# First tiles of four sequences moved to the front of a fused attention and feed-forward kernel

## The chip, the cores and the metric

The kernel runs on one core of a Trainium2 chip. The core has a matrix engine (TensorE, PE in the profile, with its weight loads shown apart as PEld), a vector engine (VectorE, DVE), a scalar engine (ScalarE, ACT), GpSimd (POOL) and SyncE (SP). The last two mostly issue transfers here. PE writes its results to PSUM; DVE and ACT read them from there. The metric is the time of one execution on the device in microseconds. Lower is better.

## The reference

Inputs are q, k and v of shape (4, 8, 768, 64): four sequences, eight heads, 768 positions, 64 values per head. Each position attends to the 96 positions up to its own and to the first 8 positions of its sequence. The result is reshaped to 3072 rows of 512 and goes through two matrix products with a squared relu between them. Output is 3072 x 512 in float32.

```
scores = scale * q @ k^T
is_global = pos[None, :] < 8
is_local = (rel >= 0) & (rel < 96)
dist = where(is_global & ~is_local, 96, abs(rel))
scores = scores - slopes[head] * dist, and -1e9 where neither holds
a = exp(scores - max); a = a / sum(a)
x = (a @ v), heads side by side: (3072, 512)
out = (relu(x @ w_in) ** 2) @ w_out        # w_in 512 x 2048, w_out 2048 x 512
```

## The kernel before

**Tiles and blocks.** The 3072 rows are 24 tiles of 128 rows, six to a sequence (TPB = 6). Two tiles make a block, twelve blocks in all. A tile of attention goes through these operations, named as in the order below (j is the tile):

- ld.q, ld.k, ld.v (or `load.j` for all three): transfers issued on POOL that also turn float32 into bf16. Tiles 0 to 5 and the weights (ld.win, ld.wout) are loaded one by one at the start, tiles 6 to 23 by `load`. q and k of tile 0 come in float32 on SP.
- tr and T (tiles 0 to 5): PE transposes q (tr.0.j) and k (tr.1.j), and ACT or DVE copies them from PSUM to `qkT`. From tile 6 on, T.j is a transposing DMA issued on SP.
- bias (tiles below NBIAS = 3): PE writes the distance bias into the PSUM bank ahead of the scores, with a scaled identity `sid` against the table `pb` or `pb0` (L530).
- sc.j.g: scores (L550). The first tile of a sequence has no left neighbour: 8 matmuls of 128 columns in one group. Every later tile takes its own keys and those of its left neighbour (which carries the 8 global keys in its first rows, put there by gk, or by kl into a copy): 16 matmuls in two groups.
- exp (ACT, L616), then mul (DVE, L641) by the table of exponentials of the bias, `E`, or `E0` for a first tile. Tiles with the bias written by PE need no mul.
- pv.j.h: two halves of matmuls with v (L703), 8 matmuls for a first tile and 16 for a later one; norm (DVE, L733 and L734) divides; gv copies the eight global rows of v into the tile's v for its right neighbour.
- trx and xT (tiles 0 to 7): x is transposed by PE and copied; from tile 8 on xT is a transposing DMA on SP.

The feed-forward part of block b has eight steps. s1.b.s (L826) multiplies x of the block by 256 columns of w_in, eight matmuls of 256 columns (for the first steps of block 0 in parts, `#2` and so on), relu.b.s (ACT, L849) and sq.b.s (ACT L865 or DVE L867) follow. The second product s2 is plain in block 0 (L1104). In blocks 1 to 11 it is done with seven products in place of eight (p1 to p7, L975), on sums of squares (sum, L932) and of weights (wsum, L896); part and o bring the results together and st stores them.

**What sets the order.** The whole program is one list of words, ORDER (L54 to L140). `Plan.run` (L38) goes through the list and emits each operation, so every engine works in the order in which its words stand there, and waits in that order. A letter behind @ chooses ACT or DVE. The costs, due times and margins in the code (LEADS, SAFE, SAFEX and the numbers in `plan.op`) belong to a planner that is not in this file; `run` does not read them.

**Buffers.** `qkT` has NKT = 12 places, v has NV = 12, each used by tile j in place j % 12. q and k as loaded have six places for the first six tiles and three (NQ) for all later ones. `ps_g` has six PSUM banks, shared by transposes, scores, pv and s1 results (hT).

Of the kernel before, what the change touches and what calls it, by code (L numbers as in the profile page):

```python
# [54 lines left out]
tr.0.0 T.0.0@A ld.k.1 tr.1.0 ld.q.1 tr.1.1 ld.v.0 bias.0.0 ld.k.2 T.1.1@V tr.0.1 T.1.0@A T.0.1@V sc.0.0 bias.1.0  # L55
sc.1.0 exp.0.1.0 tr.1.2 exp.0.0.0 ld.q.2 exp.1.1.0 bias.1.1 pv.0.0 norm.0.0 exp.1.0.0 ld.q.3 sc.1.1 ld.v.1 T.1.2@A
exp.1.1.1 tr.0.2 gk.1 tr.0.3 T.0.2@V pv.0.1 ld.k.3 exp.1.0.1 bias.2.0 sc.2.0 norm.0.1 pv.1.0 ld.v.2 tr.1.3 norm.1.0
T.0.3@A exp.2.1.0 pv.1.1 exp.2.0.0 T.1.3@V ld.win.0.1 ld.win.0.0 norm.1.1 trx.0 gv.1 ld.win.6.0 xT.0@V bias.2.1 sc.2.1
exp.2.0.1 gk.2 pv.2.0 norm.2.0 exp.2.1.1 trx.1 sc.3.0 sc.3.1 xT.1@V pv.2.1 ld.v.3 exp.3.0.0 exp.3.0.1 E0.0 s1.0.0
exp.3.1.0 s1.0.0#2 s1.0.0#3 s1.0.0#4 ld.win.3.0 s1.0.6 norm.2.1 mul.3.0.0 gv.2 ld.k.4 mul.3.1.0 trx.2 mul.3.0.1  # L60
exp.3.1.1 ld.q.4 mul.3.1.1 pv.3.0 pv.3.1 norm.3.0 norm.3.1 relu.0.0 xT.2@A relu.0.6 ld.win.4.0 s1.0.3 s1.0.3#2 gk.3
sq.0.0@A ones.6 trx.3 tr.1.4 T.1.4@A relu.0.3 ld.win.1.0 tr.0.4 xT.3@V sq.0.6@A s1.1.0 T.0.4@V s1.1.6 ld.q.5 ld.k.5
relu.1.0 s1.1.4 sq.0.3@V sq.1.0@V relu.1.6 ld.win.2.1 ld.win.2.0 gv.3 s1.0.1 sq.1.6@V relu.1.4 s1.0.1#2 sc.4.0
sq.1.4@A relu.0.1 tr.0.5 ld.wout.0 exp.4.0.0 s1.1.3 sq.0.1@V sc.4.1 T.0.5@A s1.0.4 mul.4.0.0 exp.4.1.0 ld.win.5.0 E0.1
ld.v.4 s1.0.2 relu.1.3 sq.1.3@A exp.4.1.1 gk.4 s1.1.2 ld.win.7.0 mul.4.1.0 s2.0.0.0 tr.1.5 relu.1.2 s2.0.0.1 exp.4.0.1
s1.0.2#2 s1.0.2#3 sq.1.2@V ld.v.5 T.1.5@A mul.4.0.1 s1.0.2#4 relu.0.4 ld.wout.2 s1.0.5 ld.wout.1 relu.0.2 sq.0.4@V
pv.4.0 s1.1.7 sq.0.2@A mul.4.1.1 norm.4.0 relu.0.5 relu.1.7 pv.4.1 sc.5.0 norm.4.1 sc.5.1 ld.wout.5 exp.5.0.0 sq.0.5@V
s1.1.5 sq.1.7@A gv.4 mul.5.0.0 exp.5.1.0 exp.5.1.1 s1.0.7 exp.5.0.1 ld.wout.3 relu.1.5 mul.5.1.0 trx.4 xT.4@V
mul.5.0.1 s2.0.1.0 mul.5.1.1 pv.5.0 ld.wout.4 norm.5.0 relu.0.7 s1.1.1 ld.wout.7 pv.5.1 norm.5.1 s2.0.1.1 s2.0.2.1
s2.0.2.0 s2.0.3.0 sq.1.5@V trx.5 s2.0.4.0 s2.0.5.0 s2.0.3.1 s2.0.4.1 wsum.0.0 relu.1.1 ld.wout.6 load.6 load.7 xT.5@V  # L70
sq.1.1@V s2.0.5.1 sq.0.7@A s1.2.0 relu.2.0 sq.2.0@A wsum.0.1 wsum.2.0 s2.0.6.0 sum.1.0 sum.1.1 s2.0.7.0 s1.2.3
relu.2.3 wsum.2.1 gate.8 o.0.0@A wsum.1.0 s2.0.6.1 s2.0.7.1 s1.2.6 s2.1.p1.0 T.6 relu.2.6 T.7 s1.2.7 sq.2.3@A sq.2.6@A
s1.2.5 load.8 s2.1.p1.1 sum.1.3 part.1.p1@A s1.2.4 wsum.1.1 relu.2.5 o.0.1@A s2.1.p6.0 relu.2.7 s1.2.2 st.0.1 sq.2.5@A
st.0.0 s2.1.p2.0 wsum.3.0 relu.2.2 s2.1.p2.1 s2.1.p6.1 sq.2.7@A o.1.p2 sum.1.2 relu.2.4 sc.6.0 part.1.p6@A s2.1.p5.0
exp.6.0.0 sq.2.4@V wsum.3.1 s2.1.p5.1 exp.6.1.0 sc.7.0 mul.6.0.0 sc.7.1 s2.1.p7.0 exp.7.0.0 T.8 s2.1.p7.1 gate.9
sq.2.2@A mul.6.1.0 exp.7.1.1 part.1.p7@V s1.2.1 exp.7.1.0 mul.7.0.0 pv.6.0 mul.7.1.1 o.1.p5 exp.7.0.1 norm.6.0 pv.6.1
relu.2.1 mul.7.1.0 mul.7.0.1 s2.1.p4.0 s2.1.p4.1 sq.2.1@A o.1.p4@A s2.1.p3.0 s2.1.p3.1 norm.6.1 load.9 st.1.1 pv.7.1
pv.7.0 o.1.p3 s2.2.p1.0 st.1.0 norm.7.0 trx.6 norm.7.1 s2.2.p1.1 s2.2.p2.0 xT.6@A trx.7 T.9 gk.7 sum.2.0 s2.2.p2.1
xT.7@V sc.8.0 sc.8.1 s1.3.0 s1.3.3 gate.10 sum.2.1 exp.8.0.0 exp.8.1.0 s1.3.7 part.2.p1@A relu.3.0 load.10 exp.8.0.1
gv.7 mul.8.0.0 sum.2.2 sq.3.0@A s1.3.2 exp.8.1.1 mul.8.0.1 s2.2.p6.0 mul.8.1.0 relu.3.7 s2.2.p6.1 relu.3.2 mul.8.1.1  # L80
load.11 sq.3.7@V o.2.p2 pv.8.1 pv.8.0 relu.3.3 s1.3.5 part.2.p6@A norm.8.0 s2.2.p5.0 s2.2.p7.0 sq.3.3@A sq.3.2@A gk.8
sum.2.3 relu.3.5 s2.2.p5.1 sc.9.0 norm.8.1 gv.8 xT.8 exp.9.1.0 mul.9.1.0 sc.9.1 T.10 load.12 sq.3.5@V exp.9.0.0
exp.9.1.1 mul.9.0.0 exp.9.0.1 s2.2.p7.1 s1.3.1 part.2.p7@V mul.9.1.1 s1.3.6 o.2.p5 relu.3.1 relu.3.6 s1.3.4 sq.3.1@A
pv.9.0 mul.9.0.1 s2.2.p4.0 norm.9.0 pv.9.1 norm.9.1 gk.9 s2.2.p4.1 relu.3.4 sq.3.4@A o.2.p4@A s2.2.p3.0 s2.2.p3.1
sq.3.6@A xT.9 s2.3.p1.0 load.13 o.2.p3 s2.3.p1.1 sum.3.0 s2.3.p2.0 part.3.p1@A T.11 sum.3.1 s2.3.p2.1 sum.3.2 sc.10.0
exp.10.1.0 sc.10.1 s2.3.p6.0 s2.3.p6.1 o.3.p2 exp.10.0.0 gv.9 mul.10.1.0 s2.3.p5.0 s2.3.p5.1 part.3.p6@V exp.10.0.1
mul.10.0.0 exp.10.1.1 s2.3.p7.0 mul.10.0.1 load.14 gk.10 mul.10.1.1 s2.3.p7.1 part.3.p7@A pv.10.0 pv.10.1 s1.4.0
norm.10.0 s1.4.7 norm.10.1 relu.4.0 sc.11.0 sc.11.1 s1.4.4 T.12 relu.4.7 s1.4.3 sq.4.0@V exp.11.0.0 o.3.p5 exp.11.1.1
gv.10 mul.11.0.0 exp.11.1.0 s1.4.2 sq.4.7@V exp.11.0.1 load.15 mul.11.1.0 pv.11.0 relu.4.4 mul.11.1.1 mul.11.0.1
relu.4.3 sc.12.0 sq.4.4@A sq.4.3@V s1.4.5 xT.10 st.2.0 relu.4.2 norm.11.0 exp.12.1.0 pv.11.1 s1.4.6 relu.4.5  # L90
exp.12.0.0 s1.4.1 sq.4.2@V mul.12.1.0 sq.4.5@A s2.3.p4.0 norm.11.1 mul.12.0.0 s2.3.p4.1 pv.12.0 xT.11 relu.4.6
relu.4.1 sum.3.3 sq.4.6@A sq.4.1@V T.13 s2.3.p3.0 o.3.p4@A st.2.1 sum.4.0 s2.3.p3.1 o.3.p3 pv.12.1 sum.4.1 sum.4.2
s2.4.p1.0 s2.4.p1.1 s2.4.p2.0 s2.4.p2.1 part.4.p1@A s2.4.p6.0 s2.4.p6.1 part.4.p6@A o.4.p2 s2.4.p5.0 s2.4.p5.1
s2.4.p7.0 s2.4.p7.1 norm.12.0 norm.12.1 load.16 sc.13.0 sc.13.1 s1.5.0 exp.13.1.0 xT.12 T.14 mul.13.1.0 exp.13.1.1
T.15 exp.13.0.0 sum.4.3 s1.5.3 relu.5.0 part.4.p7@A s1.5.5 mul.13.0.0 mul.13.1.1 exp.13.0.1 sq.5.0@V s2.4.p4.0 pv.13.0
s1.5.1 mul.13.0.1 pv.13.1 relu.5.5 sq.5.5@V s1.5.6 relu.5.3 relu.5.1 norm.13.0 norm.13.1 sq.5.1@A xT.13 sq.5.3@V
s1.5.2 s2.4.p4.1 s1.5.4 relu.5.6 o.4.p5 s1.5.7 s2.4.p3.0 s2.4.p3.1 relu.5.2 sq.5.6@A o.4.p4@V st.3.1 gv.13 gk.13
load.18 sq.5.2@V relu.5.4 relu.5.7 sq.5.4@V sc.14.0 sq.5.7@A o.4.p3 sc.14.1 exp.14.0.0 s2.5.p1.0 s2.5.p1.1 s2.5.p2.0
s2.5.p2.1 sum.5.0 exp.14.1.0 st.3.0 T.16 load.17 part.5.p1@A sum.5.1 exp.14.1.1 mul.14.0.0 mul.14.1.0 mul.14.1.1
s2.5.p6.0 s2.5.p6.1 sum.5.2 pv.14.0 exp.14.0.1 s1.6.1 s1.6.0 norm.14.0 part.5.p6@A kl.14 relu.6.0 mul.14.0.1 o.5.p2  # L100
kl.15 relu.6.1 s2.5.p7.0 pv.14.1 s2.5.p7.1 norm.14.1 sq.6.0@A s2.5.p5.0 part.5.p7@A xT.14 sc.15.0 sc.15.1 s2.5.p5.1
s1.6.4 s1.6.3 exp.15.0.0 sum.5.3 exp.15.1.0 s2.5.p4.0 mul.15.0.0 exp.15.0.1 gv.14 sq.6.1@V s1.6.2 s2.5.p4.1 exp.15.1.1
mul.15.0.1 mul.15.1.1 relu.6.3 mul.15.1.0 o.5.p5 st.4.0 load.19 sq.6.3@A relu.6.4 pv.15.0 s2.5.p3.0 norm.15.0 relu.6.2
pv.15.1 o.5.p4@A norm.15.1 sc.16.1 sq.6.2@V sc.16.0 xT.15 s1.6.7 s2.5.p3.1 sq.6.4@A exp.16.1.0 exp.16.0.0 mul.16.1.0
exp.16.0.1 gv.15 mul.16.0.0 T.17 s1.6.5 exp.16.1.1 relu.6.7 s1.6.6 relu.6.6 o.5.p3 s2.6.p1.0 mul.16.0.1 st.4.1
sq.6.7@A relu.6.5 pv.16.0 mul.16.1.1 sq.6.6@V pv.16.1 s2.6.p2.0 s1.7.0 sq.6.5@V sum.6.0 T.18 load.21 st.5.1 gk.16
s1.7.5 relu.7.0 relu.7.5 s2.6.p2.1 s2.6.p1.1 s1.7.1 norm.16.0 norm.16.1 xT.16 part.6.p1@A sum.6.1 sc.17.0 sc.17.1
gv.16 sq.7.0@A sum.6.3 s2.6.p6.0 s2.6.p6.1 o.6.p2 sq.7.5@A exp.17.1.0 s1.7.3 s2.6.p5.0 sum.6.2 s2.6.p5.1 relu.7.1
load.20 mul.17.1.0 exp.17.0.0 mul.17.0.0 pv.17.0 part.6.p6@A s2.6.p7.0 s1.7.2 s2.6.p7.1 sq.7.1@V exp.17.0.1 relu.7.3
# [58 lines left out]


# [1027 lines left out]
```

## Time and profile before

| what | value |
|---|---|
| median of 3 runs | 204.5 us (204.19 to 204.57) |
| profiled execution | 204.49 us, span of its instructions 202.7 us |
| PE busy | 196.9 us (97%) |
| PE weight loads busy | 166.7 us (82%) |
| DVE busy | 148.4 us (73%) |
| ACT busy | 146.1 us (72%) |
| s1 matmuls (hT, L826) in the chain of waits | 41% of the span |
| second product, blocks 1 to 11 (acc, L975) in the chain | 34% |
| scores (L550), pv (L703) in the chain | 5% each |
| from the loads at the start (POOL and DMA) in the chain | about 9% |
| load of a q, k or v tile, issue to landing, median | 4.8 to 5.6 us |
| DMA traffic | 27.38 MB, mean 135 GB/s |

How to read it: the span runs from the first to the last instruction of the profiled execution; its time has about 1.8 us more. Matmuls are pipelined, so the mean length of one (273 ns for 256 columns) is longer than the 109 ns that it keeps the engine from the next. The chain of waits goes back from the last instruction, at each step to what released it, and so gives the time that a group occupies. The table of windows gives the busy time of each engine, with counts, in stretches of the span.

### The profile page before, as it was taken

Reading aid. Unit: us, or ns where it says so; the run is one execution under the profiler, and the core shown is the slowest. Engines: PE = TensorE matmul, PEld = TensorE weight load, DVE = VectorE, ACT = ScalarE, POOL = GpSimd, SP = SyncE. Lnnn points to the kernel's source line nnn. Section 1 sums busy time; section 2 is a strip of 40 time slices with the busy share of each in tenths; the row PEclk is TensorE's granted clock in tenths of the full one; section 3 lists DMA queues with packets and bytes.
Section 4 is the critical chain, followed back from the end, with each engine's and each line's share of the span. In section 5 each row is a group of like instructions: output and inputs, shape, how many; then the busy total and the mean of one; then the engine's idle time right before and its main releaser. Section 6 shows DMA issues by size and latency. Waiting matters only on the chain.

```text
span 202.7 us, 5686 instructions
## 1 busy us (share of the span) xinstructions
PE 196.9 (97%) x2272; PEld 166.7 (82%) x2272; DVE 148.4 (73%) x404; ACT 146.1 (72%) x289; POOL 75.4 (37%) x93
## 2 busy tenths in 40 slices
...
GB/s 126 153 173 179 180 184 205 192 147 182 136 175 139 155 130 121 193 179 91 118 235 137 160 118 145 129 160 204 107 143 105 100 78 29 12 118 55 0 110 102
DMA packets 113965, 27.38 MB, mean 135 GB/s; under 512 B 105490, under 2 KB 111122, under 8 KB 113938
## 3 DMA queue, kind: packets, MB, share of 16 engines
...
## 4 chain that ended last, share of the span: by engine, by line
PE 88%; POOL 6%; DMA 3%; DVE 0%; issue 0%; POOLq 0%
PE hT L826 41%; PE acc L975 34%; PE sc L550 5%; PE po L703 5%; PE acc L1104 3%; DMA qk<-in_q_dram 3%; POOL qk L267 3%; POOL v L267 2%; POOL win L267 1%; PE tr L463 0%; PE trx L771 0%; DVE o L1051 0%; POOL pbi L327 0%; POOLq L327 0%; POOLq L1178 0%
## 5 line engine op out<-in xcount | busy, mean ns | idle before, releaser
L826 PE MATMUL hT<-xT,win 128*128 128x256 bf16 (+1 forms) x800 | 93.8, 268 | 0.0
L826 PEld LDWEIGHTS <-win 128*128 128x128 bf16 x800 | 74.0, 98 | 9.8
L849 ACT ACTIVATE hr<-hT 128x512 f32<-128x512 f32 x96 | 56.0, 605 | 20.8 <-PE hT L826 17.4
L616 ACT ACTIVATE esc<-sc 128x512 bf16<-128x512 f32 x78 | 42.5, 606 | 5.9 <-PE sc L550 5.3
L270 POOL DMA_DIRECT2D qk<-in_q_dram x18 | 16.2, 902 | 66.9 <-DMA qkT<-qk 51.3
L867 DVE TENSOR_TENSOR hs<-hr 128x512 bf16<-128x512 f32 x43 | 29.5, 685 | 15.7 <-ACT hr L849 15.5
L975 PEld LDWEIGHTS <-hsum 128*128 128x128 bf16 x360 | 33.5, 98 | 5.0 <-issue 0.6
L641 DVE TENSOR_TENSOR at<-esc,E 128x512 bf16<-128x512 bf16 x78 | 30.6, 417 | 6.7 <-ACT esc L616 6.3
L975 PE MATMUL acc<-wsum,hsum 128*128 128x256 bf16 x264 | 34.3, 273 | 0.0
L865 ACT ACTIVATE hs<-hr 128x512 bf16<-128x512 f32 x53 | 33.2, 634 | 0.7
L975 PEld LDWEIGHTS <-hs 128*128 128x128 bf16 x264 | 25.0, 98 | 2.9
L975 PE MATMUL acc<-wout,hs 128*128 128x256 bf16 x176 | 23.0, 273 | 0.0
L1051 DVE TENSOR_TENSOR o<-acc,part 128x256 f32<-128x256 f32 (+2 forms) x34 | 14.0, 411 | 10.7 <-PE acc L975 9.3
L734 DVE TENSOR_TENSOR x<-po,rs 128x256 bf16<-128x256 f32 x48 | 20.4, 424 | 1.7
L390 ACT COPY part<-acc 128x256 f32<-128x256 f32 x24 | 9.0, 374 | 15.0 <-PE acc L975 14.6
L703 PE MATMUL po<-v,at 128*128 128x65 bf16 x352 | 17.8, 194 | 0.4 <-DVE v L751 0.3
L703 PEld LDWEIGHTS <-at 128*128 128x128 bf16 x352 | 15.8, 98 | 2.2 <-issue 0.4
L270 POOL DMA_DIRECT2D v<-in_v_dram x18 | 16.4, 911 | 1.3 <-DMA wout<-in_moe_w_out_dram 1.3
L270 POOL DMA_DIRECT2D qk<-in_k_dram x18 | 16.2, 898 | 0.6 <-DMA wout<-in_moe_w_out_dram 0.6
L932 DVE TENSOR_TENSOR hsum<-hs 128x1024 bf16<-128x1024 bf16 (+1 forms) x24 | 15.4, 641 | 1.3 <-ACT hs L865 1.0
L733 DVE RECIPROCAL rs<-po 128x4 f32<-128x4 f32 x48 | 8.6, 179 | 8.7 <-PE po L703 8.2
L550 PEld LDWEIGHTS <-qkT 64*128 64x128 bf16 x312 | 9.5, 94 | 4.6 <-issue 4.0
...
## 6 DMA issues: line engine op xcount, KB each, us to landing
...
```

Source lines behind the costliest of these rows:

```text
L270: nc.gpsimd.dma_start(out=dst, in_=src)
L550: nc.tensor.matmul(out=tiles["sc", j, odd, g][:, at, :], lhsT=left[j - 1][half, pair, :] if kt else qkT[j % NKT][half, 1, pair, :], rhs=qk ...
L616: nc.scalar.activation(out=esc, in_=tiles.pop(("sc", j, odd, g)).rearrange("p a c -> p (a c)"), func=Act.Exp, scale=scale,)
L641: nc.vector.tensor_mul(at, tiles.pop(("esc", j, odd, g)), bias)
L703: nc.tensor.matmul(out=po[:, hi, :], lhsT=tiles["at", j, odd, g][:, at * P : (at + 1) * P], rhs=v_sb[kj][:, h, :], start=(i == 0), stop=(i ...
L734: nc.vector.tensor_tensor(out=x[:, 4 * hf : 4 * hf + 4, :], in0=po[:, :, :D], in1=rs.to_broadcast([P, 4, D]), op=Alu.mult,)
L826: nc.tensor.matmul(out=hT[:, c, cols], lhsT=w_in_sb[s][:, kt, c * P : (c + 1) * P], rhs=tiles["xT", blk][:, kt, cols], start=(kt == 0), st ...
L849: nc.scalar.activation(hr, tiles.pop(("hT", blk, s)), Act.Relu)
L865: nc.scalar.activation(hs, hr, Act.Square)
L867: nc.vector.tensor_mul(hs, hr, hr)
L932: nc.vector.tensor_tensor(out=t[:, i, h], in0=t[:, a, h] if isinstance(a, int) else half_a(blk, *a)[:, h], in1=t[:, b, h] if isinstance(b, ...
L975: nc.tensor.matmul(out=tiles["acc", blk, bank][:, cols], lhsT=left_[:, s], rhs=right_[:, cols], start=first and s == 0, stop=s == NSTEP - ...
```

## The change

The tiles are renumbered. Tile j now stands for position SEQ[j] of the old numbering: first the four first tiles of the sequences (0, 6, 12, 18), then all others in their old order. Blocks are pairs of the new numbers, so block 0 and block 1 hold the four first tiles, and blocks 2 to 11 hold later tiles only. Loads and stores go to the rows of SEQ[j]. The left neighbour is LEFT[j] and the first tile of the sequence HEAD[j].

The first four places of `qkT` and of v belong to the first tiles for good; the later tiles share the other eight (`ring`). NBIAS becomes 4, so the four first tiles have their bias written by PE and need no mul; E0 and its preparation on DVE are gone. relu may be on ACT or on DVE: 63 are on ACT and 33 on DVE. Of the 96 squares 66 are on ACT and 30 on DVE (before 53 and 43). ORDER is a new list throughout. SAFE and SAFEX have other values.

```diff
+    SEQ = sorted(range(NT), key=lambda i: (i % TPB > 0, i))
+    TURN = {i: j for j, i in enumerate(SEQ)}
+    HEAD = [TURN[i - i % TPB] for i in SEQ]
+    LEFT = [TURN[i - 1] if i % TPB else None for i in SEQ]
+
+    def ring(j):
+        return j if j < B else B + (j - B) % (2 * TPB - B)
...
-    NBIAS = 3
+    NBIAS = 4
...
-    v_sb = [v_ring[j % NV] for j in range(NT)]
+    v_sb = [v_ring[ring(j)] for j in range(NT)]
...
-    SETS = {j: [(0,), (1,)] for j in range(NT) if j % TPB}
+    SETS = {j: [(0,), (1,)] for j in range(NT) if SEQ[j] % TPB}
-    COPY = [14, 15, 19, 20, 22]
+    COPY = [TURN[i] for i in (14, 15, 19, 20, 22)]
...
     def src_rows(x, j):
-        b, t = divmod(j, TPB)
+        b, t = divmod(SEQ[j], TPB)
...
-    def emit_E0(e, odd):
-        cur = E[:, odd, :, :, 0, :].rearrange("p g i c -> p (g i) c")
-        left = E[:, odd, :, :, 1, :].rearrange("p g i c -> p (g i) c")
-        nc.vector.tensor_copy(E0[:, odd], cur)
-        nc.vector.tensor_max(E0[:n_global, odd], cur[:n_global], left[:n_global])
...
-        T_ = qkT[j % NKT]
-        ku = kT_users[j % NKT]
+        T_ = qkT[ring(j)]
+        ku = kT_users[ring(j)]
...
-                    lhsT=left[j - 1][half, pair, :] if kt else qkT[j % NKT][half, 1, pair, :],
-                    rhs=qkT[j % NKT][half, 0, pair, :],
+                    lhsT=left[LEFT[j]][half, pair, :] if kt else qkT[ring(j)][half, 1, pair, :],
+                    rhs=qkT[ring(j)][half, 0, pair, :],
...
-                    kjs = (j,) if first else (j, j - 1)
+                    kjs = (j,) if first else (j, LEFT[j])
...
-            nc.scalar.activation(hr, tiles.pop(("hT", blk, s)), Act.Relu)
+            hT = tiles.pop(("hT", blk, s))
+            if e == "ACT":
+                nc.scalar.activation(hr, hT, Act.Relu)
+            else:
+                nc.vector.tensor_scalar_max(hr, hT, 0.0)
...
-                r0 = (blk * 2 + sub) * P
+                r0 = SEQ[blk * 2 + sub] * P
```

The same replacement of j % NKT, j % NV, j - 1 and j - t by ring(j), LEFT[j] and HEAD[j] is made everywhere else that keys and values are used, in the lists of users too. Of ORDER, the words up to the first step of block 1 and those from the seventh tile to the eighth are:

```diff
+tr.0.0 T.0.0@V tr.1.0 T.1.0@V ld.q.1 bias.0.0 tr.0.1 ld.k.1 sc.0.0 tr.1.1 T.1.1@V T.0.1@A exp.0.1.0 bias.1.0 exp.0.0.0
+ld.q.3 tr.0.3 T.0.3@V ld.v.0 pv.0.0 pv.0.1 norm.0.0 norm.0.1 sc.1.0 ld.k.2 tr.1.2 ld.k.3 bias.2.0 ld.q.2 T.1.2@V
+exp.1.0.0 tr.1.3 exp.1.1.0 tr.0.2 ld.v.1 bias.3.0 T.1.3@A sc.3.0 ld.v.2 ld.v.3 T.0.2@V sc.2.0 ld.win.0.0 ld.win.0.1
+ld.k.4 ld.q.4 ld.win.1.0 pv.1.0 norm.1.0 exp.2.0.0 ld.k.5 ld.q.5 ld.win.3.0 exp.2.1.0 pv.1.1 exp.3.0.0 trx.0
+ld.win.4.0 xT.0@A pv.2.1 exp.3.1.0 norm.1.1 pv.2.0 trx.1 pv.3.0 ld.v.4 ld.wout.0 ld.win.5.0 ld.win.2.1 ld.win.2.0
+ld.wout.1 s1.0.0 norm.2.0 pv.3.1 s1.0.0#2 ld.v.5 ld.win.6.0 norm.2.1 ld.win.7.0 ld.wout.3 ones.6 trx.2 ld.wout.2
+norm.3.0 xT.1@A s1.0.0#3 xT.2@V ld.wout.4 s1.0.0#4 relu.0.0@A tr.1.4 T.1.4@A norm.3.1 trx.3 tr.0.4 xT.3@V sq.0.0@V
+s1.1.0 relu.1.0@V sq.1.0@V ld.wout.5 T.0.4@A sc.4.0 sc.4.1 exp.4.0.0 s1.1.1 mul.4.0.0 relu.1.1@V exp.4.1.0 ld.wout.6
+exp.4.0.1 s1.0.1 gk.4 s1.0.1#2 tr.1.5 exp.4.1.1 sq.1.1@A mul.4.1.1 T.1.5@A s1.0.3 mul.4.1.0 s1.1.3 relu.0.1@A
...
+sc.7.0 sq.2.1@A exp.6.1.1 mul.6.1.1 relu.2.4@A sc.7.1 exp.7.0.1 norm.6.0 s2.1.p7.1 part.1.p7@A pv.6.1 gk.7 s2.1.p5.1
+exp.7.0.0 mul.7.0.1 exp.7.1.1 sq.2.6@A load.9 norm.6.1 gv.6 s2.1.p4.0 load.11 s2.1.p4.1 s1.2.7 exp.7.1.0 relu.2.7@A
+o.1.p5 s2.1.p3.0 s2.1.p3.1 mul.7.1.1 o.1.p4@V pv.7.1 mul.7.1.0 mul.7.0.0 sq.2.4@A o.1.p3 pv.7.0 norm.7.0 s2.2.p1.0
```

More of the change, by code (lines that the diff above doesn't have):

```diff
@@ L54 @@
 ORDER = """
[L55 to L109, printed above, removed]
@@ new lines @@
+s1.0.2#2 gv.4 s2.0.0.1 exp.5.0.0 mul.5.0.0 s1.0.2#3 s1.0.2#4 exp.5.1.0 mul.5.1.0 relu.0.2@V exp.5.0.1 s1.1.5 s1.1.2
+trx.4 ld.wout.7 load.6 relu.1.5@V sq.1.5@V exp.5.1.1 mul.5.1.1 load.7 s1.1.6 sq.0.2@A relu.1.2@A s2.0.1.1 relu.1.6@A
+sq.1.6@A gk.5 s1.0.6 s1.0.7 pv.5.0 xT.4@A s1.1.7 sq.1.2@V mul.5.0.1 s2.0.1.0 relu.0.7@V pv.5.1 relu.0.6@V norm.5.0
+norm.5.1 s2.0.2.1 s2.0.2.0 trx.5 sq.0.7@A T.6 s2.0.3.0 xT.5@V wsum.0.1 sq.0.6@A s2.0.4.0 relu.1.7@A s1.2.5 sq.1.7@A
+s1.2.0 s1.2.2 wsum.0.0 wsum.1.0 s2.0.5.0 relu.2.0@V wsum.2.1 s1.2.1 sum.1.0 s2.0.6.0 relu.2.5@V sum.1.1 gate.8
@@ new lines @@
+s2.0.7.0 sum.1.3 sq.2.0@A s1.2.3 load.8 o.0.0@A relu.2.3@A T.7 s2.0.3.1 s2.0.4.1 s2.0.5.1 s2.1.p1.0 s2.1.p1.1 wsum.2.0
+part.1.p1@V sq.2.3@A s1.2.6 s2.0.6.1 sq.2.5@A relu.2.2@A s2.0.7.1 sq.2.2@A wsum.1.1 s2.1.p6.0 o.0.1@A wsum.3.0
+s2.1.p6.1 st.0.1 wsum.3.1 st.0.0 relu.2.1@V s2.1.p2.0 gv.5 T.8 sc.6.0 sc.6.1 relu.2.6@A s2.1.p2.1 exp.6.0.0 s1.2.4
+sum.1.2 exp.6.1.0 part.1.p6@V mul.6.0.0 exp.6.0.1 s2.1.p7.0 o.1.p2 s2.1.p5.0 mul.6.1.0 pv.6.0 mul.6.0.1 gk.6 gate.9
+sc.7.0 sq.2.1@A exp.6.1.1 mul.6.1.1 relu.2.4@A sc.7.1 exp.7.0.1 norm.6.0 s2.1.p7.1 part.1.p7@A pv.6.1 gk.7 s2.1.p5.1
@@ new lines @@
+exp.7.0.0 mul.7.0.1 exp.7.1.1 sq.2.6@A load.9 norm.6.1 gv.6 s2.1.p4.0 load.11 s2.1.p4.1 s1.2.7 exp.7.1.0 relu.2.7@A
+o.1.p5 s2.1.p3.0 s2.1.p3.1 mul.7.1.1 o.1.p4@V pv.7.1 mul.7.1.0 mul.7.0.0 sq.2.4@A o.1.p3 pv.7.0 norm.7.0 s2.2.p1.0
+sq.2.7@A norm.7.1 sum.2.0 trx.6 xT.6@A T.9 s2.2.p1.1 gate.10 load.10 s2.2.p2.0 trx.7 s2.2.p2.1 sum.2.1 sc.8.1 xT.7@A
+exp.8.0.1 exp.8.1.1 mul.8.0.1 sc.8.0 part.2.p1@A exp.8.1.0 exp.8.0.0 gv.7 s1.3.0 load.12 relu.3.0@A o.2.p2 mul.8.1.0
+s1.3.3 relu.3.3@A mul.8.0.0 sq.3.0@A s1.3.7 s1.3.5 pv.8.0 mul.8.1.1 norm.8.0 sq.3.3@A sum.2.2 pv.8.1 norm.8.1
@@ new lines @@
+s2.2.p6.0 xT.8 s2.2.p6.1 st.1.0 T.10 part.2.p6@A relu.3.5@A s1.3.2 relu.3.2@V s2.2.p7.0 s2.2.p7.1 T.11 sq.3.5@A
+sum.2.3 s2.2.p5.0 relu.3.7@V s1.3.4 sc.9.0 sc.9.1 sq.3.7@A sq.3.2@V exp.9.1.0 part.2.p7@V s1.3.1 relu.3.4@V exp.9.0.0
+exp.9.1.1 s2.2.p4.0 s2.2.p4.1 s2.2.p5.1 mul.9.1.0 mul.9.0.0 pv.9.0 relu.3.1@A mul.9.1.1 s1.3.6 exp.9.0.1 sq.3.4@A
+o.2.p5 sq.3.1@A mul.9.0.1 norm.9.0 relu.3.6@V pv.9.1 s2.2.p3.0 norm.9.1 o.2.p4@A sq.3.6@A s2.2.p3.1 o.2.p3 gk.9
+s2.3.p1.0 sum.3.0 sum.3.1 s2.3.p2.0 s2.3.p2.1 s2.3.p1.1 sc.10.0 sc.10.1 part.3.p1@V xT.9 o.3.p2 sum.3.2 s2.3.p6.0
```

168 lines of the change are left out of this document (94 added, 74 removed).

## The prediction

> **What bounds the kernel now.** I read the page's busy shares first, then busy time by stage, then the chain of waits.
>
> ```profile
> PE 196.9 (97%) x2272; PEld 166.7 (82%) x2272; DVE 148.4 (73%) x404; ACT 146.1 (72%) x289; POOL 75.4 (37%) x93
> ```
> TensorE (PE) is the bound; the others idle for a quarter of the span. By stage (window; busy time and count for each engine; granted clock; DMA):
>
> ```profile
> 5.00:15.75 10.75, 9.58 (x155) 6.97 (x156) 6.06 (x21) 8.29 (x18) 10.75 (x14) 1.00 2.19 163
> 15.75:20.77 5.02, 4.76 (x80) 4.22 (x76) 4.47 (x22) 4.16 (x9) 4.67 (x6) 1.00 1.81 181
> 20.77:50.17 29.40, 29.40 (x305) 23.12 (x303) 19.55 (x44) 22.13 (x43) 16.14 (x20) 1.00 1.72 179
> 50.17:200.05 149.88, 149.43 (x1733) 130.89 (x1730) 113.99 (x296) 108.31 (x215) 39.68 (x45) 1.00 1.08 124
> ```
> From 20.77 us on PE never pauses; only the first 20 us can be shortened by supplying it better. The chain of waits (start, length, what) says who sets the pace there, and what a group of matmuls occupies when PE is full:
>
> ```profile
> 13.22 0.74 POOL qk L267
> 13.97 6.52 DMA qk<-in_q_dram
> 20.49 0.05 issue
> 20.54 0.40 PE tr L463 x4
> 20.93 3.51 PE hT L826 x40
> ...
> 31.01 0.24 PE po L703 x8
> ...
> 32.49 0.55 PE sc L550 x16
> 33.05 1.85 PE hT L826 x16
> 34.90 0.22 PE trx L771 x4
> 35.12 0.43 PE acc L1104 x2
> ...
> 48.86 0.44 PE acc L975 x4
> 49.30 0.87 PE hT L826 x8
> 50.17 1.31 PE acc L975 x12
> ```
> The loads issued on POOL set the pace until q of tile 4 lands at 20.49; then it is PE alone. Prices: a step of the first product (s1, eight hT matmuls) 0.87, a piece of the second (p, four) 0.44 or in block 0 (two) 0.43, scores of a later tile 0.55, eight pv matmuls 0.24, a transpose of a tile 0.22. The same chain prices a group of eight score matmuls at 0.33.
>
> **The part that is certain.** A first tile has 8 score and 8 pv matmuls, a later one 16 and 16, so it is cheaper by (0.55 - 0.33) + 0.24 = 0.46 us of PE, wherever it runs. Their number does not change, only their place. Bias: before 16 matmuls of 256 columns and 8 of 128, after 32 of 128. By the timeline a group of eight of 128 takes 0.61 us, one alone 0.219, so each further one (0.61 - 0.219)/7 = 0.056; four of 256 take 0.60, one 0.273, so 0.109. That is 2.2 us before and 1.8 after: 0.4 less, all of it ahead of the first s1, where PE waits for loads.
>
> **The head, worked through.** The loads form one stream. Before, the first (k of tile 1) lands at 6.2 us, where the first transposes of it start; q of tile 4, the sixteenth, lands at 20.49. By then twelve loads of 128 KB, two halves and two wholes of w_in (768 KB) are in, 2304 KB. So the rate is (2304 - 128)/(20.49 - 6.2) = 152 KB/us, or 0.84 us for a q, k or v tile and 1.68 for a w_in step. The windows up to 40 us show 179 to 204 GB/s once whole weights dominate, about 1.35 for a step of 256 KB; I use that from w_in 4 on.
>
> After the change ten attention loads, not nine, stand ahead of w_in 0. In the new order q2 is seventh (11.3 us), v3 tenth (13.8), w_in 0 complete at 15.5, k4 16.3, q4 17.2, w_in 1 at 18.8, w_in 3 at 22.2.
>
> PE's order then binds it: tr.0.2 waits until 11.3; transpose, bias.3.0, sc.3.0 and sc.2.0 are done at about 12.7. Behind them ACT runs exp.2.0.0, exp.2.1.0, exp.3.0.0, xT.0 and exp.3.1.0 in turn, five by 0.61 (row of L616), to 15.8. pv.3.0 needs the last, and the first quarter of s1.0.0 stands behind pv.3.0 on PE: **s1 starts at 16.05**, against 15.84 before. So the six exps less ahead of block 1 do not bring it forward: the tenth load and ACT's queue take that back. After it: s1.0.0 0.9, three transposes 0.66, pv.3.1, waits for xT.3, so s1.1.0 near 18.9; s1.1.0, sc.4, s1.1.1, s1.0.1 and a transpose (0.87 + 0.55 + 0.87 + 0.87 + 0.22 = 3.4) end at 22.3, where w_in 3 has just landed. From here each weight step feeds two blocks (1.74 us of PE for 1.35 of DMA), so PE is full.
>
> Up to the place that the old kernel reached at 50.17 (all of blocks 0 and 1 in s1, seven steps of block 2, all s2 of block 0, three pieces of block 1) there remain 23 - 4 = 19 steps by 0.87 = 16.5; sixteen times 0.43 = 6.9; three times 0.44 = 1.3; a transpose of q and two of x 0.66; sc.5 0.55; four pv groups 0.96. Sum 26.9, and 0.3 for weights that land just late: **49.5, so 0.65 us are gained.**
>
> **What is given back.** At that place the old kernel has done one first tile and five later ones, the new one four and two. Three later tiles in place of three first ones remain: 3 by 0.46 = **1.4 us, now in a stage where PE is full**; in the head they ran while PE waited for loads anyway. Span 202.7 - 0.65 + 1.4 = 203.4. Around the span the profiled execution has 204.49 - 202.7 = 1.8, so **205.2 us**; the execution stands at the median of the runs, 204.5.
>
> **The other parts.** E0 goes (two copies and two maxima of rows L398 and L399, 1.5 us of DVE) and two multiplications (417 ns) come: hidden behind PE. 33 relu move from ACT (605 ns) to DVE. No row has it; nearest are the three widths of L1051, 64 columns 224 ns and 256 columns 418 on average, which is 1.0 ns a column and 0.68 us for 512, and the ACT row below. With squares, copies and transposed x moved the other way ACT changes by -33 x 0.605 + 13 x 0.634 - 5 x 0.374 + 2 x 0.6 = -12.4, to 134 us, DVE by +33 x 0.68 - 13 x 0.685 + 5 x 0.42 - 2 x 0.42 + 0.8 - 1.5 = +14, to 163 (80%). Cover is PE's work; without it each relu costs its bank, so s1 waits up to 0.68 us for one.
> The page "VectorE: DVE Perf Modes" of the Trainium skill (section "Why PSUM operands drop a tier") says that a fp32 operand in PSUM holds VectorE to one element a cycle; at the clock it states that is an estimate of 0.53 us and a start, nearer ACT's 0.605. By it DVE would have some 3 us less and the sum stays, as PE covers both.
>
> Ring: keys and values of later tiles have eight places, not twelve. load.12 then waits for pv.5, which the order has some 30 us ahead, so POOL and the loads queued behind it wait for nothing new. The bytes, the 18 tile loads, 34 transposes by DMA and the stores stay; row numbers alone change. LEADS, SAFE and SAFEX feed a planner that this file does not run: `run` emits ORDER, so they cost nothing.
>
> The new order behind 50 us I cost at nothing, with bounds. Its work by the prices before: 73 steps x 0.872 + 151 pieces x 0.437 + scores 15 x 0.55 + 3 x 0.33 + pv 15 x 0.48 + 3 x 0.24 + 0.4 = 147.2 in 149.9 us, so at most 2.7 can be won, and 0.5 of that is the wait between the last two pieces, whose order stays. Upward: sc.7 to pv.7.0 has four exps, a copy and a square on ACT (3.5 us) and two multiplications behind, under 3.75 us of PE work, a stall of 0.6; a transposed load that misses its place costs what such a DMA takes from issue to landing, 4.6 us at the median, less the 2 us that order leaves: 2.6.
>
> **Rivals.**
> (a) Faster. The new order closes the gaps behind 50 us: relu on whichever engine is free empties the hT bank sooner. For it: ACT waits and works in turns before (hr waits 17.4 us for PE in all). Against: that is ACT waiting for PE, not PE for a bank. It decides if PE's gaps of 2.7 fall below 1.3: two thirds of the open 2.2 gives 205.2 - 1.5 = 203.7. Chance 0.20.
> (b) No difference: ACT's chain at the head is shorter than worked out, s1 starts at 15.4 and the gain is 1.3, level with the 1.4: 204.5. Chance 0.20.
> (c) Slower by more: every block from 2 on now has two later tiles, eight exps and eight multiplications, with no lighter block between, and DVE at 80%; x of blocks 3 to 9 comes late by one stall of 0.6 in some and one of 2.6: 205.2 + 2 = 207.2. Against: ACT has 12 us less to do. Chance 0.25.
> (d) PE's clock drops in the emptier head. The eight first matmuls of 512 columns take 585 ns on average, later ones of that shape 379, so it starts slow; after that the windows above grant 1.00. The new head has some 7 us of work between 4.6 and 16. A stretch as long as those eight matmuls (3.27 us in the timeline) at half speed would cost 1.6: 206.8. Against: no wait in my head is over 1 us, as before. Chance 0.03.
> "TensorE: Matmul & The Clock Gate" of the Trainium skill (Part 1) says the clock is halved after an idle window of about 3.4 us; by it the clock stays, since no wait is so long.
> Forecast as worked out: 0.32.
>
> **Numbers.** About 0.2% (0.4 us) is what a measurement here tells from no change. Faster takes (a): 0.20. Same (b): 0.20. Slower the forecast, (c) and (d): 0.60. Range: low is the forecast less 0.6 in the head and 1.3 of the gaps, 203.3; high adds one stall of 2.6 to 205.2, with rounding 208. The forecast's own range is 204.9 to 206.
>
> **What would show it.** First 128-column hT matmul near 16 us; s1.1.0 near 19; p6 of block 1 complete near 49; scores and pv after that longer by 1.4 us; PE full from 50 to the end with about 2.7 us of gaps; DVE about 160, ACT about 134; relu on DVE 0.6 to 0.7. Wrong if s1 starts before 15 us, or if the windows behind 50 us gain over 1.5 us.

## The result and the profile after

The changed kernel takes 207.73 us (median of four runs, 207.35 to 207.87), the kernel before 204.43 on the same chip (204.19 to 204.57): a ratio of 1.0153, 95% interval 1.0139 to 1.0168, or 3.3 us more. The time forecast was 205.2 and the range 203.3 to 208.0. The direction is right and the range holds it, but the size is that of rival (c), 207.2. The profiled execution takes 207.71 us, its span 205.9. Of all the executions below one is left out of ratios and ranges, 209.52 us in run 9, because it lies over 2% above the fastest of its kernel.

The busy shares of the page after:

```profile
PE 197.4 (96%) x2276; PEld 167.6 (81%) x2280; DVE 163.7 (79%) x425; ACT 137.2 (67%) x266; POOL 75.3 (37%) x93
```

PE's work is the same as before to within 0.5 us (196.9), so most of the longer span is time in which PE stands still. The windows say where. They are those of the prediction, with two more inside the last one (window; busy time and count of PE, PEld, DVE, ACT and POOL; PE clock, DMA share, GB/s):

```profile
5.00:15.75 10.75, 8.74 (x140) 7.12 (x138) 7.04 (x27) 7.11 (x15) 10.75 (x13) 1.00 2.30 156
15.75:20.77 5.02, 4.30 (x60) 3.54 (x61) 3.41 (x8) 2.65 (x6) 5.02 (x8) 1.00 1.82 172
20.77:50.17 29.40, 29.19 (x306) 22.95 (x308) 21.32 (x47) 19.91 (x38) 15.84 (x20) 1.00 1.63 177
50.17:200.05 149.88, 148.56 (x1738) 129.96 (x1735) 125.67 (x318) 104.39 (x203) 39.52 (x45) 1.00 1.09 122
70.00:80.00 10.00, 9.79 (x131) 8.13 (x130) 9.05 (x28) 6.63 (x15) 5.26 (x6) 1.00 1.42 156
90.00:100.00 10.00, 8.97 (x116) 7.77 (x114) 7.91 (x22) 7.33 (x16) 2.64 (x3) 1.00 1.34 127
```

Between 5 and 20.77 us PE is busy for 13.04 us, where it was for 14.34 before: 1.3 us less, although the first s1 matmul starts earlier (15.08 against 15.84). Behind that, one stretch of ten microseconds stands out, 90 to 100, with 1.03 us idle, and a smaller one from 70 to 80. Before, both were full.

To see the loss grow, each PE operation was given the price that it has where PE is full, and at each moment the time was added to the work that was left, for both kernels. After minus before, in us:

```
at             20    50    70    75    80    90    96   140   198
lost so far  1.35  1.13  1.30  1.67  2.00  1.84  3.01  3.22  3.24
```

Three steps make it: 1.3 by 20 us, 0.6 to 0.7 around 75, 1.1 at 94 to 96. After that the kernels run level. The head in the timeline of PE after (start, length, engine, line, operation, count, and in brackets the idle time before and what ended it):

```profile
10.94 0.40 PE L459 MATMUL tr<-ident,qk 128*128 128x128 bf16 x4 [0.38 <-DMA qk<-in_q_dram]
...
14.98 0.27 PE L695 MATMUL po<-v,at 128*128 128x65 bf16 x3 [0.78 <-ACT at L612]
15.08 0.39 PE L818 MATMUL hT<-xT,win 128*128 128x128 bf16 x4
...
15.90 0.40 PE L818 MATMUL hT<-xT,win 128*128 128x128 bf16 x4 [0.31 <-DMA win<-in_moe_w_in_dram]
...
18.38 1.03 PE L818 MATMUL hT<-xT,win 128*128 128x256 bf16 x8 [0.29 <-DVE xT L403]
```

The waits are those that the prediction walked through: q of tile 2, the fifth exp of the chain (pv.3.0), then w_in and the transposes of x. The other two steps in the chain of waits after, between 60 and 110 us:

```profile
72.87 0.68 DVE hr L845
73.55 0.10 DVE rs L725
73.68 0.42 DVE x L726
74.10 0.34 DVE o L1047
74.49 1.47 PE acc L971 x12
...
87.36 0.05 issue
87.47 8.14 DMA qkT<-qk
95.66 0.62 PE sc L546 x16
```

At 74.49 PE starts the pieces s2.3.p2.0 and behind only when DVE has done four things in turn, the last of them `o`, which empties an accumulator bank; the first is a relu (0.68 us) that was on ACT before. At 95.66 the scores of tile 13 start, when the transposing DMA that feeds them has landed after 8.1 us. PE had been free since 94.63, for 1.03 us. What POOL issued meanwhile:

```profile
85.36 0.88 POOL L281 DMA_DIRECT2D qk<-in_q_dram  x1 [6.04 <-DMA qkT<-qk]
86.23 0.88 POOL L281 DMA_DIRECT2D qk<-in_k_dram  x1
87.10 0.90 POOL L281 DMA_DIRECT2D v<-in_v_dram  x1
```

These three are load.15. They landed at 88.9, 93.4 and 95.4, beside the transpose, which had been issued at 87.47.

### The profile page after: what moved, and what is told of

Its sections match the earlier page's. It is cut to its first block, busy times and chain, and to the rows that moved or that the text cites. A ratio compares the mean times of both kernels' runs of the same rounds, so it can differ in the third digit from the quotient of the medians.

```text
span 205.9 us, 5685 instructions
## 1 busy us (share of the span) xinstructions
PE 197.4 (96%) x2276; PEld 167.6 (81%) x2280; DVE 163.7 (79%) x425; ACT 137.2 (67%) x266; POOL 75.3 (37%) x93
## 4 chain that ended last, share of the span: by engine, by line
PE 67%; DMA 15%; POOL 8%; DVE 7%; issue 1%; POOLq 0%; SPq 0%
PE acc L971 30%; PE hT L818 28%; DMA wout<-in_moe_w_out_dram 8%; POOL qk L278 4%; PE sc L546 4%; PE po L695 4%; DMA qkT<-qk 4%; DMA v<-in_v_dram 3%; POOL v L278 2%; POOL win L278 2%; DVE wsum L892 2%; DVE hr L845 1%; DVE hsum L928 1%; DVE o L1047 1%; DVE hs L863 1%
## 5 line engine op out<-in xcount | busy, mean ns | idle before, releaser
L818 PE MATMUL hT<-xT,win 128*128 128x256 bf16 (+1 forms) x800 | 95.1, 268 | 0.7 <-DMA win<-in_moe_w_in_dram 0.3
L843 ACT ACTIVATE hr<-hT 128x512 f32<-128x512 f32 x63 | 37.4, 600 | 19.8 <-PE hT L818 17.0
L861 ACT ACTIVATE hs<-hr 128x512 bf16<-128x512 f32 x66 | 40.5, 634 | 12.8 <-DVE hr L845 12.0
L633 DVE TENSOR_TENSOR at<-esc,E 128x512 bf16<-128x512 bf16 x80 | 31.7, 418 | 4.5 <-ACT esc L612 3.5
L971 PE MATMUL acc<-wsum,hsum 128*128 128x256 bf16 x264 | 35.0, 273 | 0.1
L845 DVE TENSOR_SCALAR hr<-hT 128x512 f32<-128x512 f32 x33 | 22.4, 686 | 7.3 <-PE hT L818 4.1
L971 PE MATMUL acc<-wout,hs 128*128 128x256 bf16 x176 | 23.5, 273 | 0.2 <-DVE o L1047 0.2
L863 DVE TENSOR_TENSOR hs<-hr 128x512 bf16<-128x512 f32 x30 | 20.4, 685 | 2.3 <-ACT hr L843 2.0
L695 PEld LDWEIGHTS <-at 128*128 128x128 bf16 x352 | 15.4, 98 | 3.8 <-ACT at L612 1.9
L401 ACT COPY part<-acc 128x256 f32<-128x256 f32 x19 | 7.2, 378 | 10.0 <-PE acc L971 10.0
```

What stands on the lines that cost most here:

```text
L633: nc.vector.tensor_mul(at, tiles.pop(("esc", j, odd, g)), bias)
L695: nc.tensor.matmul(out=po[:, hi, :], lhsT=tiles["at", j, odd, g][:, at * P : (at + 1) * P], rhs=v_sb[kj][:, h, :], start=(i == 0), stop=(i ...
L818: nc.tensor.matmul(out=hT[:, c, cols], lhsT=w_in_sb[s][:, kt, c * P : (c + 1) * P], rhs=tiles["xT", blk][:, kt, cols], start=(kt == 0), st ...
L843: nc.scalar.activation(hr, hT, Act.Relu)
L845: nc.vector.tensor_scalar_max(hr, hT, 0.0)
L861: nc.scalar.activation(hs, hr, Act.Square)
```

## The experiments

The theory: 1.3 to 1.4 us come from moving three later tiles out of a head that cannot use the room into a stage where PE is full, 1.1 from the transpose of tile 13 that runs beside load.15, and 0.6 from DVE's queue in block 3. The rivals are named with each run. Ratios are to the kernel before on the same chip.

**1 and 2. What a tile's attention costs in the head, and where PE is full.** In the kernel before, three tiles are made as cheap as first tiles: 1, 2 and 3 in run 1, 8, 9 and 10 in run 2.

```diff
+    LIGHT = {1, 2, 3}
...
-        first = t == 0
+        first = t == 0 or j in LIGHT
```

The words of their second groups (sc.j.1, exp.j.0.1, exp.j.1.1 and, where the tile has them, the two mul) leave ORDER, in run 1 also bias.1.1 and bias.2.1.

> The kernel before, with tiles 1, 2 and 3 leaving out their left neighbour (8 score and 8 pv matmuls, two exps and, for tile 3, two multiplications less each; the result of these rows is another). By the prices of the prediction 3 x 0.46 = 1.4 us of PE work go, and 0.2 us of bias, all in the first 20 us. Theory (PE waits for loads there, attention work in the head is nearly free): 204.4 falls by 0.6 or less, to 203.8 to 204.4. Rival (work costs the same wherever it runs): falls by 1.4 to 1.6, to 202.9.

Measured: 204.89 us, ratio 0.9999 (0.998 to 1.0018), profiled span 202.5. That fits the theory (a fall of 0.6 us or less) and not the rival (1.4 to 1.6). Between 5 and 20 us PE has 1.8 us less to do, and the time stays. Two lines of that kernel's trace, one from the windows and one from the timeline, show why:

```profile
5.00:20.00 15.00, 11.90 (x180) 9.62 (x178) 9.30 (x39) 9.41 (x19) 15.00 (x19) 1.00 2.04 162
```

```profile
20.19 0.40 PE L463 MATMUL tr<-ident,qk 128*128 128x128 bf16 x4 [0.21 <-DMA qk<-in_q_dram]
```

PE is busy for 11.90 of 15 us, before 13.73, and still waits for q of tile 4, at 20.19 instead of 20.54. POOL, which issues the loads, is busy without a pause.

> The kernel before, with tiles 8, 9 and 10 leaving out their left neighbour in the same way (in the stretch from about 65 to 100 us). Theory (PE is full there and has no slack): 204.4 falls by the full 1.4 us, to 203.0. Rival (such work is hidden there or an other engine paces): falls by under 0.7. The difference between this run and light_head is the price of moving three later tiles from the head into the full stage; theory 0.8 to 1.4 us, rival 0.

Measured: 203.66 us, ratio 0.9955 (0.9931 to 0.9979), 0.9 us less, between the two expectations; the profiled span is 201.8, and in it 1.24 of the 1.4 us are kept (the kernel enters block 2 0.36 us later than before and ends 0.88 earlier). PE is full where they run, with 108 matmuls in a window that holds 126 before:

```profile
60.00:70.00 10.00, 10.00 (x108) 8.48 (x106) 7.51 (x21) 7.64 (x15) 7.98 (x9) 1.00 1.79 159
```

So the attention of three such tiles, with its work on ACT and DVE, is worth nothing in the head and about 0.9 us in the full stage. The change moved such work from the first place to the second.

**3. load.15 held back.** One DVE write into its buffer, behind norm.12.1, makes it wait until tile 13's transpose has started.

```diff
-            if NFIRST + 2 + NQ - 1 <= j < JGATE:
+            if NFIRST + 2 + NQ - 1 <= j < JGATE or j == 15:
...
-pv.12.0 norm.12.0 sq.4.4@A load.15 pv.12.1 s1.5.3 s1.5.0 norm.12.1 sq.4.7@A load.16
+pv.12.0 norm.12.0 sq.4.4@A pv.12.1 s1.5.3 s1.5.0 norm.12.1 gate.15 load.15 sq.4.7@A load.16
```

> The kernel after, with the load of tile 15 held back (a small write by DVE behind norm.12.1, near 92.8 us, which the load must wait for; it was issued at 85.4). Theory (the transposed load of tile 13, issued at 87.5, takes 8.1 us because the loads of tile 15 run beside it, and sc.13 waits for it with PE idle 1.2 us): the transposed load of tile 13 lands before 93 us, PE's gap before sc.13 goes, and the time falls by 1.0 to 1.3 us to 206.5. Rival (two transposed loads in a row and the one of x before them are slow by themselves): it still lands after 95 us and the time stays at 207.7.

Measured: 207.09 us, ratio 1.011 (1.008 to 1.014). The transpose issued at 87.6 now takes 4.7 us. Its line between 80 and 100 us (three transposes; issue to landing), first of the kernel after, then of this one:

```profile
DMA to landing us min/median/max: 3.1/7.5/8.1
```

```profile
DMA to landing us min/median/max: 4.1/4.7/4.9
```

and in the chain of waits of this kernel PE goes into the scores of tile 13 without a pause:

```profile
92.14 1.75 PE hT L818 x16
93.88 0.87 PE acc L971 x8
94.76 0.55 PE sc L546 x16
```

The gap is gone. By the ratios the gain is 0.9 us (1.0153 to 1.011, intervals that just touch), by the remaining-work account 0.97, a little under the theory's 1.0 to 1.3. The rival is out: the two transposed loads and the one of x still follow each other as before.

**4. The scores moved away from the late transpose.** The load stays, and other work is put in front.

```diff
-sum.4.3 sc.13.1 exp.13.0.1 sc.13.0 s2.4.p6.0 s2.4.p6.1 relu.5.3@V s1.5.7 mul.13.0.1
+sum.4.3 s2.4.p6.0 s2.4.p6.1 relu.5.3@V s1.5.7 sc.13.1 exp.13.0.1 sc.13.0 mul.13.0.1
```

> The kernel after, with the scores of tile 13 (and one exp) moved in the order behind s2.4.p6 and s1.5.7, 1.74 us of PE work that does not need them; loads untouched. Theory (only PE's place in the order makes the late load cost time): the gap of 1.2 us goes and the time falls by 0.9 to 1.3 us to 206.6. Rival (the exps, multiplications and pv of tile 13, now 0.5 us later, make the next wait): falls by under 0.5 us.

Measured: 209.65 us, ratio 1.0223 (1.0189 to 1.0257), slower than after, where both expectations had it fall. The gap is not gone but further on, in its timeline (DVE, the weight loads of PE, PE):

```profile
97.68 0.43 DVE L633 TENSOR_TENSOR at<-esc,E 128x512 bf16<-128x512 bf16 x1 [2.14 <-ACT esc L612]
...
98.69 0.68 DVE L928 TENSOR_TENSOR hsum<-hs 128x1024 bf16<-128x1024 bf16 x1
...
99.43 0.33 PEld L971 LDWEIGHTS <-hsum 128*128 128x128 bf16 x4 [1.49 <-DVE hsum L928]
99.43 0.61 PE L971 MATMUL acc<-wsum,hsum 128*128 128x256 bf16 x4 [1.21 <-ACT esc L612]
```

PE stands at s2.4.p7.0, which needs two things. The copy part.4.p6 of its bank ends on ACT at 98.89. Its weights are sum.4.2, which DVE ends last, at 99.37; the row of the weight loads names it, while the row of the matmul names an exp that only ended at about that time. On DVE sum.4.2 stands behind two multiplications of tile 13, and the first of these waited 2.14 us for an exp of tile 13, which now starts 1 us later than in the kernel after (97.05, not 96.09). Moving a wait on one engine in a fixed order moves all that stands behind it on the others. The profiled execution, 208.40 us, is the fastest of the six and shows 0.6 of the 1.4 us by which the ratio is above that of after; the rest is in no trace.

**5. All relu back on ACT.** 33 words relu.b.s@V become @A; 22 squares go to DVE in exchange.

```diff
-s1.1.0 relu.1.0@V sq.1.0@V ld.wout.5 T.0.4@A sc.4.0 sc.4.1
+s1.1.0 relu.1.0@A sq.1.0@V ld.wout.5 T.0.4@A sc.4.0 sc.4.1
```

> The kernel after, with all 96 relu on ACT as in the kernel before, and for the 22 steps whose relu leaves DVE and whose square was on ACT, the square on DVE. DVE falls by 33 x 0.686 - 22 x 0.685 = 7.6 us, ACT rises by 33 x 0.600 - 22 x 0.634 = 5.9. Theory (PE covers either engine, except in block 3): within 0.5 us of 207.7. Rival (relu on DVE is what makes the stage behind 50 us slow): falls by over 1 us. Second rival (the order was made for relu where it stands, so each engine's queue is now wrong): rises by over 1 us.

Measured: 212.26 us, ratio 1.0375 (1.0352 to 1.0398). The page has DVE at 156.5 us (74%) and ACT at 141.6 (67%), so DVE is back near its share of before (73%), and still PE waits in many places. The longest wait behind its first matmul is for a copy that stands on ACT behind a relu:

```profile
20.50 0.23 PE L546 MATMUL sc<-qkT 64*128 64x128 bf16 x2 [1.16 <-ACT qkT L401]
```

The second rival came true: in this order, moving the relu back costs 4.5 us. That fits an order made for their places. It does not show what relu on DVE cost in an order made for them on ACT, which was not run.

**6. Block 3 alone.** One relu goes to ACT, and the piece p1.1, whose bank is free, goes ahead of p2.0.

```diff
-relu.3.6@V
+relu.3.6@A
...
-s2.3.p1.0 sum.3.0 sum.3.1 s2.3.p2.0 s2.3.p2.1 s2.3.p1.1 sc.10.0
+s2.3.p1.0 sum.3.0 sum.3.1 s2.3.p1.1 s2.3.p2.0 s2.3.p2.1 sc.10.0
```

> The kernel after, with relu.3.6 on ACT and the second group of p1 of block 3 ahead of p2 (as the kernel before has it). Theory (0.37 us of PE before p2.0 and its 0.2 after it are the time that o.2.p3 stands behind relu.3.6 and norm.9.1 on DVE): the gap goes, 0.3 to 0.6 us less, 207.2. Rival (the second group of p1 waits for its last square instead): under 0.2 less.

Measured: 207.27 us (206.09 to 208.49), ratio 1.0123 (1.0089 to 1.0156), 0.6 less than after, though the intervals overlap. The gap at 74 is gone: 70 to 80 us is full (10.00 of 10.00), and DVE now stands idle for 0.23 us before `o`. By the remaining-work account the stretch still loses 0.4 of 0.7 us: the step before 75 is gone, the one between 75 and 80 is not. The two edits were not run apart. The profiled execution was the longest of its runs (208.49 us), and its timeline has a wait that after's does not have:

```profile
142.32 0.93 PE L818 MATMUL hT<-xT,win 128*128 128x256 bf16 x7 [0.76 <-DMA xT<-x]
```

The chain of waits names the transfer, again a transpose beside loads that had been issued from 129 us on:

```profile
135.22 6.97 DMA xT<-x
142.19 0.14 issue
```

In after's profile the same transpose takes 5.5 us and lands just in time. This execution also has PE wait 0.84 us for w_in at 23.07, ahead of all that the edits touch, where after's has no wait. So a transfer that is in time in one execution can be late in another. With one trace for each kernel, how often is not shown.

**7. w_in earlier in the head.** The first weights load ahead of v of tiles 2 and 3, and s1.0.0 goes ahead of pv.2 and pv.3.

```diff
-sc.3.0 ld.v.2 ld.v.3 T.0.2@V sc.2.0 ld.win.0.0 ld.win.0.1 ld.k.4
+sc.3.0 ld.win.0.0 ld.win.0.1 ld.v.2 ld.v.3 T.0.2@V sc.2.0 ld.k.4
...
-exp.3.0.0 trx.0 ld.win.4.0 xT.0@A pv.2.1 exp.3.1.0 norm.1.1 pv.2.0 trx.1 pv.3.0
+trx.0 xT.0@A exp.3.0.0 norm.1.1 trx.1 s1.0.0 s1.0.0#2 ld.win.4.0 pv.2.1 exp.3.1.0 pv.2.0 pv.3.0
```

> The kernel after, with both halves of w_in 0 loaded ahead of v of tiles 2 and 3, and in the order xT.0 ahead of exp.3.0.0, trx.1 and the first two quarters of s1.0.0 ahead of pv of tiles 2 and 3. Theory (the tenth load ahead of w_in 0 and the queue of ACT hold s1 back in the head): s1.0.0 starts near 14.3 instead of 15.1 us and the head gains 0.4 to 0.9, time 206.9 to 207.3. Rival (v2 and v3, later by 1.7 us, hold up tiles 2 and 3 and s1.1.0 by as much): s1.1.0 stands at 18.4 or later and the time is within 0.3 of 207.7 or above it.

Measured: 207.76 us, ratio 1.0156 (1.0134 to 1.0177): no gain. s1 starts 1 us earlier and the next block later, in its timeline:

```profile
14.12 0.61 PE L818 MATMUL hT<-xT,win 128*128 128x128 bf16 x8
...
16.07 0.40 PE L695 MATMUL po<-v,at 128*128 128x65 bf16 x8 [1.11 <-DMA v<-in_v_dram]
...
18.77 0.94 PE L818 MATMUL hT<-xT,win 128*128 128x256 bf16 x7 [0.29 <-DVE xT L403]
```

The rival came true: v of tile 3 is late by what w_in gained. POOL issues loads without a pause here (15.00 of 15.00 us between 5 and 20), so another order of them chose only who waits.

**8. Runs 3, 6 and 7 together.**

> The kernel after with three edits at once: the load of tile 15 held back, relu.3.6 and p1 of block 3 as in block3, w_in 0 early as in win_early. Theory (three separate stalls that add up): 1.0 + 0.4 + 0.5 less, 205.8; still 1.2 to 1.4 us above the kernel before, the attention work that moved into the full stage. Rival (mending one stall opens the next): above 206.6.

Measured: 206.40 us, ratio 1.0083 (1.0065 to 1.0101). It comes between the two expectations. Both gaps are closed in its windows:

```profile
70.00:80.00 10.00, 10.00 (x135) 8.42 (x133) 8.86 (x27) 7.45 (x16) 5.32 (x6) 1.00 1.30 150
90.00:100.00 10.00, 10.00 (x126) 8.73 (x125) 8.98 (x25) 7.81 (x16) 5.35 (x6) 1.00 1.13 130
```

1.4 us of the 3.1 are recovered (1.0153 to 1.0083, intervals apart), as much as 0.9 and 0.6 of runs 3 and 6 together. 1.7 remain. In this run's trace the remaining-work account ends at 1.9: 1.25 of it by 50 us, which is the head and the moved attention, 0.2 from there to 70, 0.36 between 70 and 80 although PE counts as busy there, and 0.1 later.

**9. The same with tiles 8, 9 and 10 cheap as in run 2.** The diff is that of run 2 on top of run 8.

> The kernel after with the three repairs together (load.15 held back, block 3 mended, w_in first), and tiles 8, 9 and 10, which run where PE is full, treated as first tiles: their left neighbour is left out (8 score and 8 pv matmuls, two exps and two multiplications less for each). Theory (what is left of the loss is the dear attention that stands in the full stage, 1.4 us): 206.4 - 1.2 = 205.2 us, about 0.5 above the kernel before, so that repairs and attention together account for all but 0.5 of the 3.3. Rival (what is left is a loss spread over the order, and PE's lighter tiles only lengthen waits for exps or transposed loads): 206.0 or more.

Measured: 206.09 us (205.05 to 207.35), ratio 1.0051 (1.0024 to 1.0077). The time is that of the rival, 206.0 or more, but the kernel before stood higher on this chip as well (204.82). By the ratio 0.65 us come of the 1.2 hoped for, and with the two intervals it can be anything from 0.0 to 1.3. Part of the rest is seen in its timeline, a wait at block 3 that run 8 hardly has:

```profile
78.09 0.30 PE L695 MATMUL po<-v,at 128*128 128x65 bf16 x4 [0.41 <-DVE at L633]
```

With less PE work in between, PE seems to meet the multiplications of tile 10 before DVE is done. In the new order the attention taken away brings about half of its PE work, in the old one about two thirds; the two intervals overlap, so the difference isn't settled.

No run was faster than the kernel before except run 2, with its lighter tiles; run 1 is level with it.

## Why the prediction was right in direction and short in size

**Bound and head: right in the gain, not in every step.** s1 was forecast at 16.05, no earlier than before (15.84). It started at 15.08, so that step was wrong. The scores of tiles 2 and 3 were ready 0.3 us sooner, and ACT's five operations took 2.55 us (12.37 to 14.92), not five by 0.61: back to back they start about 0.5 us apart, less than each one lasts. s1.1.0 was forecast near 18.9, measured 18.38; s1.0.3 at 22.3, measured 22.04. The place reached before at 50.17 was forecast at 49.5. After's last piece of p6 of block 1 is done at 49.12, with one step less and one piece more done than there; 49.12 + 0.87 - 0.44 = 49.55. So 0.62 was gained of the 0.65 forecast. That it comes so near is in part luck: s1.0.3 was 0.26 us early, and the stretch behind it took 27.5 us, not 27.2. That s1 starts earlier was worth nothing by itself: run 7 moves it by 1 us and gets nothing.

**The 1.4 us given back: the mechanism is shown.** Runs 1 and 2 price three such tiles at 0.0 in the head and at 0.9 us (0.4 to 1.4) in the full stage by the ratios, 1.24 in the trace. The remaining-work account at 50 us has 1.13 lost, against 0.75 forecast (1.4 less 0.65). A later tile is dearer than a first one by 0.51 us at the prices of the full stage (0.55 and 0.48 against 0.28 and 0.24), not by 0.46, which is 0.15 of the difference; the rest was not taken apart. The 0.4 us less of bias were not run by themselves; run 1, which drops some bias too, says that work in that stretch is worth nothing.

**"The new order behind 50 us I cost at nothing": this step failed.** It was the term of the sum that was mis-sized: it cost 2.1 us (3.24 - 1.13), and that is nearly the whole distance from the forecast, 205.2, to 207.7. The pieces of it had been listed as upward bounds, with the wrong places, and left out of the sum:

- A transposed load that misses its place was bounded at 4.6 us from issue to landing less 2 us of room. At tile 13 the room was 7.2 us (87.47 to 94.63) and the transfer took 8.1, so PE lost 1.03 us idle, about 1.1 in all. Both terms were too small, and only their difference made the bound hold. Run 3 shows the cause: without load.15 beside it 4.7 us. The median was the wrong figure for this; the trace of before already had transposes of tiles up to 7.9 us, without PE waiting.
- A stall of 0.6 was put at sc.7 to pv.7.0. It is not there. 0.6 to 0.7 was lost in block 3, where `o` stood on DVE behind a relu and a norm. Run 6 closes the gap in front of p2.0, about half of this by the account; the other half is not explained.
- The 2.7 us that could have been won behind 50 us were not won, so rival (a) was wrong.

**Engines.** DVE was forecast at 163 us and is 163.7; ACT at 134 and is 137.2; the 3 us between were not taken apart. A relu on DVE was priced at 0.68 and takes 0.686, as the page after has it:

```profile
L845 DVE TENSOR_SCALAR hr<-hT 128x512 f32<-128x512 f32 x33 | 22.4, 686 | 7.3 <-PE hT L818 4.1
```

The Trainium skill, "VectorE: DVE Perf Modes", section "Why PSUM operands drop a tier", gave the prediction an estimate of 0.53 us and a start. The trace decides: 0.686 us, so by the page's rate the start would be some 0.15 us, an estimate too.

**"Cover is PE's work" was right for most relu and wrong for one.** In block 3 the relu stood ahead of `o`, and PE was the next in line. Run 5 shows only that taking all relu off DVE does not mend this order.

**Rivals.** (c) was near in price, 207.2, and right in its mechanism in part: a stall of 0.6 and one of a transposed load. They came in blocks 3 and 4, once each, the second with 1.1 us and not 2.6, and not as x that comes late in blocks 3 to 9, so the near price is in part luck. So is it that the range holds 207.73: its upper end stood on the one stall of 2.6. Its share of DVE, 80%, came true without being the bound. (b) needed s1 at 15.4: it came at 15.08, and the gain by 50 us was still 0.62, not 1.3; that s1.1.0 and not s1 sets the pace fits run 7. (d) did not happen: the granted clock is 1.00 in all windows above. "TensorE: Matmul & The Clock Gate" of the Trainium skill (Part 1) has the clock halved after an idle window of about 3.4 us; no wait of PE in any trace here is longer than 1.21 us, so the traces agree but do not test it.

**What stays open.** Run 8 is still 1.7 us above before. The account of its trace has 1.25 by 50 us; of the rest 0.36 lies between 70 and 80 us and was not taken apart. The expected return of run 9 came by half only, and its interval is too wide to say how much of that is the order. Why the same transpose takes 5.5 us in one execution and 7.0 in another was not tried, nor was an order with relu all on ACT.
